# Moving the low-part subtractions of an attention and MLP kernel from GpSimd to VectorE

## The chip, the core and the metric

The kernel runs on one core of a Trainium2 chip. A core has four engines that matter here: TensorE (PE in the profile) multiplies matrices into PSUM; VectorE (DVE), ScalarE (ACT) and GpSimd (POOL) do elementwise work. Each engine takes its instructions in the order in which the program lists them, and waits at the head of its queue for what the instruction needs. SyncE (SP) issues most of the DMAs. The metric is the device time in microseconds; lower is better.

## What is computed

Attention over hashed buckets (2 batches, 8 heads, 768 tokens, 64 columns a head), then an MLP with squared ReLU (1536 tokens, 512 to 2048 to 512), then a mixture of 8 experts in which tokens are assigned greedily, 192 to each expert.

```python
def _attn_ref(q, k, v, proj):
    ...
    scores = scale * np.matmul(q, k.transpose(0, 1, 3, 2))
    scores = np.where(mask, scores, -1000000000.0)
    ...
    return np.matmul(attn, v).astype(np.float32)

def _moe_ref(x, w_in, w_out):
    h = np.maximum(x @ w_in, 0.0)
    return (h * h @ w_out).astype(np.float32)

def _moe2_ref(x, w_gate, w1, w2):
    logits = x @ w_gate
    order = np.argsort(-logits.flatten())
    ...
    for e in range(E):
        mask = assigned == e
        h = np.maximum(x[mask] @ w1[e], 0.0)
        out[mask] = h @ w2[e]
```

## The kernel before

Matrix products run in a rounded 32-bit type. To keep accuracy, each operand x is split into a high part hi, x rounded by ScalarE, and a low part lo = x − hi, and a product is the sum of three: hi·hi, hi·lo and lo·hi. `halve` (line 819) is the split of the MLP: its step 0 is the high part on ScalarE (line 821), its step 1 the low part, a subtraction of two SBUF operands on GpSimd (line 823).

The MLP works in 32 steps that the code calls slices s, listed in SEQ: each is one block f of 128 hidden columns (16 blocks) for one batch b of 768 tokens. `load` and `conv` (lines 798 and 803) bring a weight block and bring its 64-bit numbers into float32: L809 on ScalarE, then L811, L813, L815 and L817 on VectorE, each on 1024 columns. `split` (line 828) halves the three pieces of a block: 512 columns of w_out and two pieces of 256 of w_in.

The first 14 slices (PLAIN = 14) are plain: `first` multiplies (L874), evicts with ScalarE (L881) and VectorE (L883), and halves the hidden values (`chain`, line 876), 384 columns at a time. From slice 14 on slices go in pairs by a Strassen-like scheme with seven products for eight (`pairs`, L898), which needs sums of tokens and sums of weights. `tokens(b)` makes the token sums of batch b: for each of two column groups eight additions on VectorE (`tsum`, L861, in the tile tz) and four splits (`thalf`, line 863). `sums` (L841) makes the weight sums, whose split has 1024 columns. The products of a pair are evicted by L903 (ScalarE) and L905 (VectorE), squared by ScalarE (L909), halved by `chain`, and all slices go on to the second product (`mlp2`, L922). L939 adds up its results over the runs of SEQ.

Attention (L582 to L659) stands before the MLP, the router (L1312 to L1730, some of it already during the last slices) and the experts (L1877 to L2095) behind it.

No order is written out by hand. Each step goes to a planner, `Sched.add`, with its engine, a duration, what it depends on and a priority, lower first. `order` (line 107) plays the steps through on the engines, always starting what can start first, and emits the instructions of each engine in that order. A step with `port=True` may not run beside another such step in this play (line 150); GpSimd steps have it by default, of the VectorE steps the sums, and of the conversions only some. The real engines wait only for data, not for these marks. The priority of a slice's step of kind k is 500 + 10·s + MP[k] (line 986); tables like it (PR, EP, RP, FP) serve the other parts.

Of the kernel before, what the change touches and what calls it, by code (L numbers as in the profile page):

```python
# [232 lines left out]
XV = 8  # L233
XC = -13
PREP, PW, DL = -40.5, 0.8, 2.4
PREP1 = -10.5
LDP = (2, 0)
PR = {"S": 22, "mx": 1810, "ex": 846, "dn": -3872, "rec": -1060.5, "nrm": 1123.5, "tp": 28, "hi": -477.5, "lo": 542.5, "pv": 30, "oa": -524.5, "od": -1775, "pe": -35.5, "pa": -810.5, "pd": -1926}


def host_consts_a():
# [475 lines left out]
NS, STAG = 32, 3  # L717
PLAIN = 14
HALF = SEQ[PLAIN][1] + 1
MB = 500  # L720
LEAST = 3.4332275390625e-05
MP = {"ac": -17.5, "h1": -1100, "h2": 164.5, "ch": -3758, "hw": 146.5, "we": -678, "wn": -1359, "cv": -572.5, "sp": -2046.5, "sm": -72.5, "xs": -552, "sq": -3240.5, "lg": -473.5, "ev": -184.5, "lv": 292, "c0": 7498, "c1": 6337.5, "b0": 322, "b1": 3220.5}


def mlp(nc, S, ps, mem, ident, xhi, xlo, w_in, w_out, w_gate, wgt, x2d, L, att):
# [63 lines left out]
    def wo(f):  # L789
        return piece(S.unit(T["wo", f], "wo"), [512])  # L790
# [25 lines left out]
        else:  # L816
            V.scalar_tensor_tensor(x, x, LEAST, t.bitcast(F32), op0=OP.is_ge, op1=OP.mult)  # L817

    def halve(x, hi, lo, j):
        if j == 0:  # L820
            nc.scalar.activation(hi, x, AF.Copy)  # L821
        else:
            nc.gpsimd.tensor_tensor(lo, x, hi.bitcast(F32), op=OP.subtract)  # L823

    def flat(*a):
        return [x.rearrange("p " + "abc"[:len(x.shape) - 1].replace("", " ") + " -> p (" + "abc"[:len(x.shape) - 1].replace("", " ") + ")") for x in a]

    def split(f, k, j):
        if k == 2:
            halve(m(f)[:, 1], *wo(f), j)  # L830
        else:
            halve(m(f)[:, 0, 256 * k:256 * k + 256], *flat(*win(f, k)), j)

    def stg(p):
        return mem(S.unit(T["st", p], "wt"), [4, 2, 128])
# [40 lines left out]
    def chain(s, hf, j):  # L876
        hh, hl = hs(s)
        sl = slice(384 * hf, 384 * hf + 384)
        r = rs(s)[:, sl]
        if j == 0:  # L880
            nc.scalar.activation(r, hbank(s, hf), AF.Relu)  # L881
        elif j == 1:
            nc.vector.tensor_tensor(r, r, hbank(s, hf), op=OP.mult)  # L883
        else:
            halve(r, hh[:, sl], hl[:, sl], j - 2)

    def wbank(s, k):
        return ps(S.unit(T[k, s], "B"))[:, 0:384]
# [100 lines left out]
    def give(r, u, deps):  # L989
        S.add("NONE", 0.0, None, deps, rel=[(r, u)])  # L990

    def first(s):
        hd = []
        for hf in range(2):
            a = T["h", s, 0] if hf else None
            for c in range(4):
                a = S.add("PE", .52, lambda s=s, hf=hf, c=c: mlp1(s, hf, c), [*Wd[SEQ[s][1]], *[i for e in ends[4 * SEQ[s][0]:4 * SEQ[s][0] + 4] for i in e], a], prio=p(s, "h1") + hf, acq="B" if c == 0 else ())
                if c == 0:
                    T["h", s, hf] = a
                    T.setdefault(("l1", s), a)  # L1000
            L1.setdefault(SEQ[s][0], []).append(a)
            used.setdefault(SEQ[s][1], []).append(a)
            a = S.add("ACT", .37, lambda s=s, hf=hf: chain(s, hf, 0), [a, T.get(("hu", s))], prio=p(s, "ch"), acq=() if hf else ("h", "r0" if s < 2 else "r"))
            T.setdefault(("hu", s), a)
            b = S.add("DVE", .47, lambda s=s, hf=hf: chain(s, hf, 1), [a], prio=p(s, "ch"), rel=[("B", T["h", s, hf])])
            c = S.add("ACT", .41, lambda s=s, hf=hf: chain(s, hf, 2), [b], prio=p(s, "ch"))
            d = S.add("POOL", .956, lambda s=s, hf=hf: chain(s, hf, 3), [c], prio=p(s, "ch"))
            hd.append([c, d])
        give("r0" if s < 2 else "r", T["hu", s], [d, hd[0][1]])
        H[s] = hd  # L1010

    def tokens(b):

        out = {i: [] for i in range(1, 5)}
        pr = p(PLAIN, "xs") + 3 * (b == SEQ[PLAIN - 1][0])
        for c in range(2):
            A, V = {}, {}

            def add(j, deps):
                A[j] = S.add("DVE", .47, lambda c=c: tsum(b, c, j), deps, prio=pr, port=True)  # L1020

            def split2(i, deps):
                h = S.add("ACT", .41, lambda c=c: thalf(b, c, i, 0), deps, prio=pr)
                V[i] = S.add("POOL", .956, lambda c=c: thalf(b, c, i, 1), [h], prio=pr)
# [12 lines left out]
            add(6, [A[5], V[1]])
            add(7, [A[6]])
            split2(4, [A[7], *(used[HALF] if b == SEQ[PLAIN - 1][0] else ())])
            tfree[:] = [V[3], V[4], V[2]]  # L1040
        return out

    def pairs(s):
# [36 lines left out]
        for i, hf, d in ((0, 0, e2), (0, 1, z2), (1, 1, e4), (1, 0, e5)):  # L1080
            a = d if d == e5 else S.add("ACT", .41, lambda i=i, hf=hf: square(s + i, hf, AF.Relu), [d], prio=p(s, "sq"))
            a = S.add("ACT", .41, lambda i=i, hf=hf: square(s + i, hf, AF.Square), [a], prio=p(s, "sq"))
            h = S.add("ACT", .41, lambda i=i, hf=hf: chain(s + i, hf, 2), [a], prio=p(s, "ch"))
            l = S.add("POOL", .956, lambda i=i, hf=hf: chain(s + i, hf, 3), [h], prio=p(s, "ch"))
            H.setdefault(s + i, [None, None])[hf] = [h, l]
        for i in range(2):
            give("r", T["hu", s + i], [x[1] for x in H[s + i]])
# [86 lines left out]
    for f in range(16):  # L1174
# [6 lines left out]
        d = S.add("DMA", 2.9, None, [a], prio=MB + 10 * s, lat=1.8)  # L1181
        T["tm", f] = a = S.add("ACT", .95, lambda f=f: conv(f, 0), [d, *gate], prio=p(s, "cv"), acq=("wt", "mi", "mo"))
        for j in range(1, 5):
            a = S.add("DVE", dur[j - 1], lambda f=f, j=j: conv(f, j), [a], prio=p(s, "cv"), port=f < 2 or j == 1, rel={3: [("wr", T["wr", f])], 4: [("wt", T["tm", f])]}.get(j, ()))
        T["cv", f] = a

        def parts(key, n, fn, deps, sm=(), acq=()):
            i = S.add("ACT", .2 + .00073 * n, lambda: fn(0), deps, prio=p(s, "sp"), acq=acq)
            T.setdefault(key, i)
            return [i, S.add("POOL", .1 + .00225 * n, lambda: fn(1), [i, *sm], prio=p(s, "sp"))]  # L1190

        def win_(f, k, key):
            Wd[f] += parts(key, 256, lambda j: split(f, k, j), [a], acq=() if key in T else key[0])
# [13 lines left out]
        else:  # L1207
# [1002 lines left out]
```

## Time and profile before

| | us |
|---|---|
| median of three runs | 794.42 (793.69 to 794.68) |
| the profiled execution | 796.18 |
| its span, first to last instruction | 794.4 |
| TensorE busy | 762.6 |
| VectorE busy | 575.5 |
| ScalarE busy | 460.6 |
| GpSimd busy | 432.0 |

Busy time is the time in which an instruction of the engine runs. The mean granted TensorE clock is 0.972 of full speed. TensorE has two speeds, 1.2 and 2.4 GHz; a granted clock below 1.00 in a stretch says that part of it ran at the lower. Stages by time: attention to about 270, the MLP from about 250 to 560, the router to about 590, the experts to the end.

### The profile page before, as it was taken

The page shows a single profiled execution, that of the slowest core. Times are in us where ns is not written, and L with a number is a line of the kernel's source. Part 1 is how long each engine was busy: PE and PEld are TensorE (multiplying, and loading weights), DVE is VectorE, ACT ScalarE, POOL GpSimd, SP SyncE. Part 2 cuts the span into 40 slices and gives each one's busy share as a digit, 9 for nine tenths or more (in the row PEclk, how much of TensorE's full clock was granted, in tenths as well). Part 3 has the DMA queues.
Part 4 walks back from the last instruction along what each step waited for, and adds up shares of the span by engine and source line. Part 5 has one row for each costly group of instructions (what it writes and reads, how often), then busy time and mean ns, then how long its engine had stood idle before and what let it go on. Part 6 is the DMA issues. An engine that isn't in the chain of part 4 may idle for free.

```text
span 794.4 us, 14089 instructions
## 1 busy us (share of the span) xinstructions
PE 762.6 (96%) x4970; PEld 666.9 (84%) x4970; DVE 575.5 (72%) x1173; ACT 460.6 (58%) x949; POOL 432.0 (54%) x446
## 2 busy tenths in 40 slices
PE   8899999999999989999799999999999999999996
PEld 5678888888887889988688999898679899888885
DVE  6879999999999787499867666316876768754432
ACT  7789999999997663543457565544332312333332
POOL 3668778778798776576837665317421412231110
PEclk9999999999999999999999999998689999999998
DMA  8969659556701312210202310101166385897001
GB/s 181 238 131 196 131 113 190 130 120 144 178 12 54 105 54 67 93 54 29 78 22 84 106 54 1 65 15 67 68 206 208 117 277 191 306 334 267 21 8 33
DMA packets 77734, 94.34 MB, mean 119 GB/s; under 512 B 29632, under 2 KB 56640, under 8 KB 77664
## 3 DMA queue, kind: packets, MB, share of 16 engines
q1 hardware_dynamic: 75616, 87.16, 39.8%
q0 software_dynamic: 2048, 6.29, 2.6%
q8 instruction: 39, 0.64, 0.3%
q14 instruction: 31, 0.25, 0.1%
HBM read 63.55 MB, written 6.29 MB: 88 GB/s over the span
## 4 chain that ended last, share of the span: by engine, by line
PE 67%; DVE 13%; issue 8%; ACT 5%; POOL 3%; DMA 2%; SPq 1%; POOLq 0%; ACTq 0%; DVEq 0%
PE psS L922 9%; PE psS L582 7%; PE psS L1959 6%; PE psTP L898 4%; PE psO L898 4%; PE psTP L618 3%; DVE tz L861 3%; PE psm L922 2%; PE psTP L922 2%; PE psS L2000 2%; PE psO L874 2%; PE psTP L874 2%; PE psm L618 2%; PE psO L618 2%; PE psTP L639 1%
## 5 line engine op out<-in xcount | busy, mean ns | idle before, releaser
L823 POOL TENSOR_TENSOR r<-f,r 128x384 fp32r<-128x384 f32 (+3 forms) x112 | 137.5, 1251 | 106.0 <-ACT r L821 79.7
L610 POOL TENSOR_TENSOR f<-f 128x768 f32<-128x768 f32 x96 | 142.8, 1489 | 26.4 <-PE psTP L618 11.1
L922 PE MATMUL psS<-r 128*128 128x512 f32 x384 | 103.9, 406 | 0.2 <-DVE f L939 0.2
L598 DVE TENSOR_REDUCE f<-psS 128x1 f32<-128x768 f32 x96 | 90.5, 944 | 1.8 <-PE psS L582 1.6
L582 PE MATMUL psS<-r 128*128 128x384 f32 x384 | 88.1, 350 | 2.6 <-issue 1.6
L601 ACT ACTIVATE f<-psS,f 128x768 f32<-128x768 f32 x96 | 87.7, 913 | 3.4 <-DVE f L598 1.2
L922 PEld LDWEIGHTS psS<-r 128*128 128x128 f32 x384 | 73.8, 196 | 13.5 <-DVE f L939 0.5
L821 ACT ACTIVATE r<-f 128x384 fp32r<-128x384 f32 (+3 forms) x112 | 56.2, 532 | 37.4 <-DVE f L817 19.0
L1959 PE MATMUL psS<-ff,rf 128*128 128x192 f32 x400 | 76.5, 336 | 0.0
L1903 POOL DMA_INDIRECT ff<-x2d,ix x16 | 24.5, 1528 | 89.9 <-DVE ix L1728 49.9
L582 PEld LDWEIGHTS psS<-r 128*128 128x128 f32 x384 | 65.2, 188 | 8.7 <-ACT f L601 6.1
L1959 PEld LDWEIGHTS psS<-ff,rf 128*128 128x128 f32 x400 | 66.0, 193 | 1.6 <-DVE ff L1930 0.3
L2082 POOL DMA_INDIRECT out_dram<-ff,ix x16 | 16.6, 1035 | 89.5 <-DVE ff L2093 67.2
L630 DVE TENSOR_TENSOR p<-psTP,p 128x384 fp32r<-128x384 f32 x92 | 49.7, 546 | 2.9 <-ACT p L626 2.0
L626 ACT ACTIVATE p<-psTP 128x384 fp32r<-128x384 f32 x92 | 45.1, 502 | 10.7 <-PE psTP L618 9.0
L1879 DVE TENSOR_TENSOR ff<-rf,ff 128x1024 fp32r<-128x1024 f32 x22 | 26.9, 1222 | 32.5 <-ACT ff L1877 32.5
L1877 ACT ACTIVATE ff<-rf 128x1024 fp32r<-128x1024 f32 x22 | 23.3, 1057 | 45.5 <-PE psS L2030 36.3
L618 PE MATMUL psTP<-ident,f 128*128 128x128 f32 x276 | 45.1, 274 | 1.6 <-POOL f L610 1.2
L618 PEld LDWEIGHTS psTP<-ident,f 128*128 128x128 f32 x276 | 33.7, 140 | 7.9 <-issue 1.8
L909 ACT ACTIVATE f<-f 128x384 f32<-128x384 f32 x63 | 31.7, 520 | 13.4 <-DVE f L905 12.9
L604 POOL TENSOR_SCALAR f<-f 128x1 f32<-128x1 f32 x96 | 22.6, 235 | 30.5 <-ACT f L601 25.2
L874 PE MATMUL psTP<-r 128*128 128x384 f32 x150 | 29.7, 347 | 3.6 <-DVE f L883 3.6
(454 smaller groups left out, 1956.2 us busy)
## 6 DMA issues: line engine op xcount, KB each, us to landing
rf<-in_moe_w_dram SPq DMA_DIRECT2D x60, 512.0 KB, 6.4
r<-r SPq DMA_DIRECT2D x90, 192.0 KB, 4.2
f<-in_moe_w_in_dram SPq DMA_DIRECT2D x16, 512.0 KB, 3.8
f<-in_moe_w_out_dram SPq DMA_DIRECT2D x16, 512.0 KB, 4.6
r<-r SPq DMA_DIRECT2D x15, 384.0 KB, 4.0
f<-in_q_dram SPq DMA_DIRECT2D x8, 384.0 KB, 5.7
f<-in_k_dram SPq DMA_DIRECT2D x8, 384.0 KB, 6.3
f<-in_v_dram SPq DMA_DIRECT2D x8, 384.0 KB, 4.7
```

The lines of the kernel that those rows point to most:

```text
L582: nc.tensor.matmul(sbank(u)[:, hf, 0:384], T["q", (pr, h)][:, n, 128 * i:128 * i + 128], T["k", (pr, h)][:, n, 384 * hf:384 * hf + 384], s ...
L598: nc.vector.tensor_reduce(col(0, u), sbank(u)[:, :, 0:384], axis=AX.XY, op=OP.max, negate=True)
L601: nc.scalar.activation(P(u).rearrange("p (a b) -> p a b", a=2), sbank(u)[:, :, 0:384], AF.Exp, bias=col(0, u), accum_out=col(1, u))
L610: nc.gpsimd.tensor_tensor(Pn(u), P(u), col(3, u).to_broadcast([128, 768]), op=OP.mult)
L618: nc.tensor.transpose(tp(u, g)[:, j], Pn(u)[:, 128 * c:128 * c + 128], ident)
L630: nc.vector.tensor_tensor(tl, tp(u, g), th.bitcast(F32), op=OP.subtract)
L821: nc.scalar.activation(hi, x, AF.Copy)
L823: nc.gpsimd.tensor_tensor(lo, x, hi.bitcast(F32), op=OP.subtract)
L874: nc.tensor.matmul(hbank(s, hf), w[:, c % 2], y[:, x, sl], start=(c == 0 and i == 0), stop=(c == 3 and i == 2))
L898: nc.tensor.matmul(wbank(s, k), w[x][:, c], y[z][:, c], start=st and c == i == 0, stop=c == 1 and i == 2, skip_group_check=not st)
L922: nc.tensor.matmul(abank(i), a[:, t], w, start=(f == RUNS[r][1][0] and j == 0), stop=(f == RUNS[r][1][-1] and j == 2))
L1959: nc.tensor.matmul(abank(n)[:, j], raw(p, g)[:, 0, 256 * c + 128 * j:256 * c + 128 * j + 128], xT(p)[:, c], start=(c == 0), stop=(c == 3))
```

## The change

Low parts go to VectorE instead of GpSimd in three places: the hidden values of slices from 14 on (LOS), the weight pieces and weight sums of blocks from 10 on (WLO), and all token sums. The planner's durations for them change with the engine, and they are marked as users of the port, as are now all steps of a conversion. The token sums of batch b get the due time of that batch's first paired slice (14 and 18); before, both had that of slice 14, batch 1 three units behind. All tables of priorities (PREP1, PR, MP, EP, RP, FP) have new numbers; of MP this core shows all.

```diff
+LOS, WLO = 14, 10
...
-MP = {"ac": -17.5, "h1": -1100, "h2": 164.5, "ch": -3758, "hw": 146.5, "we": -678, "wn": -1359, "cv": -572.5, "sp": -2046.5, "sm": -72.5, "xs": -552, "sq": -3240.5, "lg": -473.5, "ev": -184.5, "lv": 292, "c0": 7498, "c1": 6337.5, "b0": 322, "b1": 3220.5}
+MP = {"lw": -774.5, "ac": 24.5, "h1": -252.5, "h2": 273.5, "ch": -3545, "hw": 253.5, "we": -1093, "wn": -1773, "cv": -742, "sp": -3335.5, "sm": -1005, "xs": -292.5, "sq": -2724, "lg": -93.5, "ev": 307.5, "lv": 292, "c0": 8976.5, "c1": 6037.5, "b0": 230.5, "b1": 3618}
...
-    def halve(x, hi, lo, j):
+    def halve(x, hi, lo, j, e=None):
         if j == 0:
             nc.scalar.activation(hi, x, AF.Copy)
         else:
-            nc.gpsimd.tensor_tensor(lo, x, hi.bitcast(F32), op=OP.subtract)
+            (e or nc.gpsimd).tensor_tensor(lo, x, hi.bitcast(F32), op=OP.subtract)
...
+    def we(f):
+        return nc.gpsimd if f < WLO else nc.vector
+
     def split(f, k, j):
         if k == 2:
-            halve(m(f)[:, 1], *wo(f), j)
+            halve(m(f)[:, 1], *wo(f), j, we(f))
         else:
-            halve(m(f)[:, 0, 256 * k:256 * k + 256], *flat(*win(f, k)), j)
+            halve(m(f)[:, 0, 256 * k:256 * k + 256], *flat(*win(f, k)), j, we(f))
...
     def thalf(b, c, i, j):
-        halve(tf((None, 1, 2, 0, 1)[i]), *(x[:, c] for x in tb(b, i)), j)
+        halve(tf((None, 1, 2, 0, 1)[i]), *(x[:, c] for x in tb(b, i)), j, nc.vector)
...
-            halve(r, hh[:, sl], hl[:, sl], j - 2)
+            halve(r, hh[:, sl], hl[:, sl], j - 2, nc.gpsimd if s < LOS else nc.vector)
...
+    def low(s, hf, deps):
+        pool = s < LOS
+        return S.add("POOL" if pool else "DVE", .956 if pool else .43, lambda: chain(s, hf, 3), deps, prio=p(s, "ch" if pool else "lw"), port=True)
...
-        pr = p(PLAIN, "xs") + 3 * (b == SEQ[PLAIN - 1][0])
+        pr = p(next(i for i in range(PLAIN, NS) if SEQ[i][0] == b), "xs")
...
-                V[i] = S.add("POOL", .956, lambda c=c: thalf(b, c, i, 1), [h], prio=pr)
+                V[i] = S.add("DVE", .47, lambda c=c: thalf(b, c, i, 1), [h], prio=pr, port=True)
...
-            l = S.add("POOL", .956, lambda i=i, hf=hf: chain(s + i, hf, 3), [h], prio=p(s, "ch"))
+            l = low(s + i, hf, [h])
...
-            a = S.add("DVE", dur[j - 1], lambda f=f, j=j: conv(f, j), [a], prio=p(s, "cv"), port=f < 2 or j == 1, rel={3: [("wr", T["wr", f])], 4: [("wt", T["tm", f])]}.get(j, ()))
+            a = S.add("DVE", dur[j - 1], lambda f=f, j=j: conv(f, j), [a], prio=p(s, "cv"), port=True, rel={3: [("wr", T["wr", f])], 4: [("wt", T["tm", f])]}.get(j, ()))
...
-            return [i, S.add("POOL", .1 + .00225 * n, lambda: fn(1), [i, *sm], prio=p(s, "sp"))]
+            return [i, S.add("POOL" if f < WLO else "DVE", .1 + .00225 * n if f < WLO else .05 + .00105 * n, lambda: fn(1), [i, *sm], prio=p(s, "sp"), port=True)]
...
-            Sd[q] = parts(("wS", q), 1024, lambda j, q=q: halve(*flat(stg(q), *wS(q)), j), [x, T["wx", q]])
+            Sd[q] = parts(("wS", q), 1024, lambda j, q=q: halve(*flat(stg(q), *wS(q)), j, we(2 * q + 1)), [x, T["wx", q]])
```

## Rows read from the trace of the kernel before

**Rows 1.** Busy us (instructions) of PE, PEld, DVE, ACT, POOL; clock, DMA share, GB/s.

```profile
60.00:240.00 180.00, 179.33 (x1170) 160.10 (x1169) 169.56 (x350) 167.96 (x375) 146.04 (x164) 1.00 0.62 133
270.00:295.00 25.00, 22.88 (x116) 21.41 (x116) 19.37 (x22) 14.50 (x31) 16.17 (x20) 0.94 0.25 85
295.00:340.00 45.00, 45.00 (x229) 41.00 (x228) 28.25 (x30) 21.47 (x44) 27.96 (x24) 1.00 0.21 71
340.00:402.00 62.00, 55.05 (x257) 48.33 (x256) 57.31 (x61) 26.96 (x56) 46.44 (x34) 0.94 0.15 52
402.00:480.00 78.00, 77.80 (x390) 69.98 (x389) 53.10 (x62) 48.48 (x97) 46.88 (x36) 1.00 0.20 68
480.00:540.00 60.00, 59.74 (x330) 53.60 (x329) 19.98 (x35) 28.29 (x58) 21.49 (x18) 1.00 0.08 29
540.00:590.00 50.00, 48.51 (x526) 35.13 (x525) 38.09 (x105) 21.02 (x41) 27.23 (x24) 0.73 0.27 91
```

**Rows 2.** Waits, whole execution: who waited for whom, us in total, times, longest.

```profile
PE psTP L874 <- DVE f L883: 3.9, 4, 2.1
PE psTP L898 <- ACT f L903: 3.1, 1, 3.1
PE psTP L898 <- DVE f L905: 2.0, 1, 2.0
ACT f L821 <- DVE tz L861: 17.9, 9, 4.7
```

**Rows 3.** Timelines of four engines, 382 to 388: start, us, instruction, idle before it.

```profile
383.69 1.97 POOL L823 TENSOR_TENSOR f<-tz,f 128x384 fp32r<-128x384 f32 x1
385.69 1.15 DVE L861 TENSOR_TENSOR tz<-tz,r 128x384 f32<-128x384 f32 x2 [0.89 <-POOL f L823]
386.87 0.52 ACT L821 ACTIVATE f<-tz 128x384 fp32r<-128x384 f32 x1 [4.68 <-DVE tz L861]
387.83 0.69 PE L898 MATMUL psTP<-f,r 128*128 128x384 f32 x1 [3.13 <-ACT f L903]
```

**Rows 4.** Busy VectorE us (count) of L861, L841, L813, L815 alone, 340 to 402.

```profile
340.00:402.00 62.00, 21.11 (x20) 0.94 0.15 52
340.00:402.00 62.00, 5.88 (x7) 0.94 0.15 52
340.00:402.00 62.00, 5.88 (x3) 0.94 0.15 52
340.00:402.00 62.00, 5.87 (x3) 0.94 0.15 52
```

**Rows 5.** Three lines' instructions, whole execution: shortest/median/longest in ns.

```profile
L861 DVE TENSOR_TENSOR tz<-tz,r x12: 546/888/2155, 287.2 to 394.2; 128x384 f32<-128x384 f32 x12
L841 DVE TENSOR_TENSOR f<-f x20: 409/649/1395, 355.2 to 487.2; 128x256 f32<-128x256 f32 x20
L813 DVE SCALAR_TENSOR_TENSOR f<-f x16: 1214/1921/2868, 237.4 to 478.6; 128x1024 int32<-128x1024 int32 x16
```

**Rows 6.** GpSimd's groups, 340 to 402, token sums: count, busy us, mean ns, idle before.

```profile
L823 POOL TENSOR_TENSOR f<-tz,f 128x384 fp32r<-128x384 f32 x9 | 14.3, 1593 | 1.9 <-ACT f L821 1.8
L823 POOL TENSOR_TENSOR r<-tz,r 128x384 fp32r<-128x384 f32 x3 | 5.3, 1770 | 0.0
```

**Rows 7.** GpSimd's groups, 402 to 480, in the same columns.

```profile
L823 POOL TENSOR_TENSOR r<-f,r 128x384 fp32r<-128x384 f32 x20 | 28.2, 1430 | 20.7 <-ACT r L821 10.7 <-PE psTP L898 5.2 <-issue 4.7
L823 POOL TENSOR_TENSOR r<-f,r 128x1024 fp32r<-128x1024 f32 x3 | 7.2, 2408 | 5.1 <-ACT r L821 5.1
L823 POOL TENSOR_TENSOR r<-f,r 128x512 fp32r<-128x512 f32 x5 | 6.7, 1332 | 6.8 <-ACT r L821 6.8
L823 POOL TENSOR_TENSOR r<-f,r 128x256 fp32r<-128x256 f32 x8 | 6.0, 758 | 0.0
```

**Rows 8.** Two of VectorE's groups, 402 to 480, in the same columns.

```profile
L815 DVE SCALAR_TENSOR_TENSOR f<-f 128x1024 int32<-128x1024 int32 x6 | 9.4, 1575 | 0.2
L905 DVE TENSOR_TENSOR f<-psTP,f 128x384 f32<-128x384 f32 x8 | 4.4, 552 | 11.9 <-PE psTP L898 9.4 <-ACT f L903 2.5
```

More of the change, by code (lines that the diff above doesn't have):

```diff
@@ L235 @@
 PREP, PW, DL = -40.5, 0.8, 2.4
-PREP1 = -10.5
+PREP1 = 3
 LDP = (2, 0)
-PR = {"S": 22, "mx": 1810, "ex": 846, "dn": -3872, "rec": -1060.5, "nrm": 1123.5, "tp": 28, "hi": -477.5, "lo": 542.5, "pv": 30, "oa": -524.5, "od": -1775, "pe": -35.5, "pa": -810.5, "pd": -1926}
+PR = {"S": 22, "mx": 1264, "ex": -144, "dn": -3726, "rec": -2216.5, "nrm": 1537.5, "tp": 27.5, "hi": -226, "lo": 175, "pv": 29.5, "oa": -1881.5, "od": -1440.5, "pe": -31.5, "pa": -522, "pd": -2310}
 def host_consts_a():
@@ L1006, in first @@
             c = S.add("ACT", .41, lambda s=s, hf=hf: chain(s, hf, 2), [b], prio=p(s, "ch"))
-            d = S.add("POOL", .956, lambda s=s, hf=hf: chain(s, hf, 3), [c], prio=p(s, "ch"))
+            d = low(s, hf, [c])
             hd.append([c, d])
@@ L1242, in mlp @@
     return [ld[n] for n in range(12)], st, [i for f in range(16) for i in [*Wd[f], *Sd.get(f // 2, [])]], zone_(L1[0])
-EP = {"fr": -48.5, "lr": -962.5, "row": 360, "col": -240, "cp": -71.5, "ca": 1048, "gp": 330}
+EP = {"fr": -277, "lr": -125, "row": -996.5, "col": 1318, "cp": -12, "ca": 817.5, "gp": 1047}
 CP = (5, 2, 4, 2, 1, 0)
@@ L1252 @@
 ND = 4
-RP = {"fr": 1566.5, "se": -5127.5, "oh": -545.5, "G": 3844.5, "A": 2231, "lr": 310.5, "pf": -940.5, "id": 161, "gp": 2059, "sq": 30.5, "G1": 2135.5, "A1": -374, "ei": -381, "up": 1389.5}
+RP = {"fr": 2161.5, "se": -5096.5, "oh": -968.5, "G": 3516, "A": 2902.5, "lr": 1192.5, "pf": -346.5, "id": 443.5, "gp": 2614, "sq": 196, "G1": 1462.5, "A1": -62.5, "ei": -284.5, "up": 1188.5}
 ACT_TILES = {12: (10, 11), 9: (8,), 6: ()}
@@ L1832, in squeeze @@
         st["L"], st["alive"], st["tok"] = a, None, e1
-FP = {"ga": -278.5, "xp": 2407.5, "xe": 2225, "m1": 2482, "re": -1938.5, "m2": 979, "ye": -532.5, "yt": 1964.5, "yo": 1379, "sc": 1112.5, "sp": 1289, "mr": 1136.5}
+FP = {"ga": -1074.5, "xp": 2624, "xe": 2280.5, "m1": 2986.5, "re": -1156.5, "m2": 1829, "ye": -1710.5, "yt": 2599.5, "yo": 2225.5, "sc": 1064, "sp": 545, "mr": 2334}
 AP = 5
```

## The prediction

> **What bounds the kernel now.** I read the table by stage first [rows 1]. PE is the long pole everywhere: in attention it works 179.33 of 180 us, from 295 to 340 all of 45, from 402 to 540 all but 0.5 of 138. No other engine can make those stretches shorter, only longer. Time is lost in two stretches of the MLP. From 340 to 402 PE works 55.05 of 62 us and its clock is granted at 0.94, so part of the stretch ran at the lower of its two levels: 62 − 55.05 = 6.95 us idle plus 0.06 × 62 = 3.7 us of clock, 10.7 us in all. From 270 to 295 it is 2.1 us idle plus 0.06 × 25 = 1.5 us, 3.6 us in all. The other place where PE is slow, 540 to 590 (clock 0.73), is the router, a chain of small steps that the change does not move.
>
> Then the list of waits [rows 2]: PE waits for evictions, L883 and L905 on VectorE and L903 on ScalarE, and ScalarE for L861, the token sums on VectorE. In order of time around the longest gap [rows 3]: a low part of a token sum ran on GpSimd from 383.69 for 1.97 us; VectorE sat idle 0.89 us until it ended, then ran four sums; ScalarE stood 4.68 us with a token high part at the head of its queue, behind which the eviction L903 was waiting; PE started 3.13 us late. So in 340 to 402 the chain runs through VectorE and GpSimd, and VectorE is at 57.31 of 62 us, 92%.
>
> Last, why VectorE is so full. The table by line gives 21.11 us for 20 sums, 1.06 us each, 5.88 for three L813, 5.87 for three L815, 5.88 for seven L841 [rows 4], while the shortest of them take 0.546, 1.214 and 0.409 us [rows 5] (L815 is shaped as L813, and I take its 1.214). The excess is 21.11 − 10.9 = 10.2, 2.2, 2.2 and 3.0, together 17.6 us. GpSimd's low parts are stretched too: those of token sums take 1593 to 1770 ns [rows 6]. The operations of both engines named here have two inputs in SBUF; the eviction L905, with one in PSUM, stays at 552 ns [rows 8]. The Trainium skill ("SBUF — State Buffer", Who interferes with whom) says that such a VectorE instruction and a GpSimd one exclude each other for a whole instruction; the 0.89 us of rows 3 agrees.
>
> **The change, part by part.** *Token sums.* All 16 low parts leave GpSimd; 12 of them are in 340 to 402, 9 × 1.593 + 3 × 1.770 = 19.6 us of GpSimd's 46.44 [rows 1, 6]. VectorE pays 12 × 0.546 = 6.6 us (a sum of the same shape, both inputs in SBUF). If the excess goes with GpSimd's time, 19.6/46.44 of 17.6 = 7.4 us comes back, net −0.8 us of VectorE. The ends: nothing comes back (+6.6), all of it does (−11.0). I take −0.8, since 58% of GpSimd's time in this stretch stays (slices below 14, weights below 10). On the chain itself the step gets shorter, 1.6 us on GpSimd to 0.55, and crosses between engines once less.
>
> *Their due time.* Batch 1's sums were due 3 units after batch 0's; a slice is 10 units, and now they are due with slice 18 instead of 14. Of 32 sums 20 start in the stretch [rows 4]; batch 0 goes first, so the 16 of batch 1 are all among them, at 0.546 to 1.06 us each 8.7 to 16.9 us of VectorE that no longer stands ahead of the first pair. What is late next is slice 18: the first pair starts near 383 [rows 3] and 18 slices run to 540, 8.7 us each, so the sums get some 35 us more, into 402 to 420, where VectorE still has room (53.10 of 78 [rows 1]).
>
> *Hidden and weight low parts.* From 402 to 480 GpSimd runs 36 low parts, nearly all of which move: 20 of 384 columns, 3 of 1024, 5 of 512, 8 of 256 [rows 7]. On VectorE, with 0.68 for 512 read off the line between the others (an estimate): 20 × 0.546 + 3 × 1.214 + 5 × 0.68 + 8 × 0.409 = 21.2 us. Against it stands the excess there: 6 × (1.575 − 1.214) = 2.2 us for L815 [rows 5, 8], about as much for each of the two other long steps of a conversion, some for L841: 8 us, an estimate from that row. From 480 on VectorE has 40 idle us of 60 [rows 1]; 16 moved parts fit.
>
> *The sum on VectorE, as a check.* 340 to 480: 57.3 + 53.1 = 110.4 us now; −7.4 − 8 + 6.6 + 21.2 gives 122.8. At the 92% at which it ran flat out, that is 133 us where there are 140: VectorE lets the stage shrink by about 7 us, not by the whole 10.7. I take 7.0, with ends 0 (the excess stays: 138 us) and 10.7.
>
> *270 to 295.* No low part is moved here. The 3.9 us of waits for L883, the longest 2.1 [rows 2], come where three sums stood ahead of it. The sums are now due later (xs −552 to −292.5) and conversions sooner. I take half of 3.6, 1.8 us; ends 0 and 3.6.
>
> *Turns.* More VectorE steps are marked as users of the shared port, so the planner no longer lays them beside GpSimd's. That only orders each queue, and adds no wait between the engines. I cost it at nothing beyond the above; the excess that could go with it is in the ends.
>
> *New order elsewhere.* All tables of due times are new. In attention there is nothing to win (0.7 us of 180) and up to 2 us to lose, by the nearest row of a disturbed stretch, 270 to 295. Router and experts keep their work: 0, ends ±3 us, about the size of the stage losses above. No DMA is moved; the expert weights start when the MLP closes, and so move with it.
>
> **Sum.** −7.0 − 1.8 = −8.8 us. The profiled execution took 796.18 us, 794.4 of it span: 787.4. The median of the runs is 794.42, 1.8 lower, so on that scale 785.6, which I predict.
>
> **Rivals.** *The turns work and all comes back* (13%): 10.7 + 3.6, and a few us of the router's 0.73 clock because GpSimd is free earlier: −14 to −17, 777.5 to 780. For it: 52 token and hidden low parts leave GpSimd, and those of six weight slices. Against: the check sum.
>
> *The change does not do what it says* (15% for a small gain, 8% for none): order is no wait, conversions and the low parts left on GpSimd go on meeting, the excess stays, and only the later due time helps: −1.6 to −5, 789.4 to 793, or nothing, 794.4. The Trainium skill ("Perfetto Trace Analysis", Optimizing Scalar/DVE Operations) warns that moving work between the two might not help because they share a read port; the stretched rows agree that they share it, but a VectorE low part would hold it for 0.55 us and a GpSimd one runs 1.43 [rows 5, 7].
>
> *VectorE becomes the bound from 402 to 480* (17%, slower): 53.1 − 8 + 21.2 = 66.3 us there, and with batch 1's 16 sums and 8 low parts (24 × 0.546 = 13.1) 79.4 of 78. Evictions L905 then stand behind conversions in one queue, the next pair's banks come free late, and PE idles. It decides once VectorE passes the 92% of 340 to 402; by that stretch's own loss, 10.7 of 62, it costs 17% of 78 = 13.4 us. With 8.8 won before it: +4.6, 799. The Trainium skill ("Perfetto Trace Analysis", Optimizing Scalar/DVE Operations) advises taking work off a saturated VectorE, which speaks for this rival. Against: half of batch 1's part can run before 402, which gives 72.8, and 295 to 340 has 16 us of VectorE idle.
>
> **How the numbers follow.** Forecast (−5 to −12) 47%, larger 13%, small gain 15%, none 8%, slower 17%. About 0.2%, 1.6 us, is what can be told from no change: faster 0.75, same 0.08, slower 0.17. For 8 in 10 the range takes in the larger gain and no change, and leaves the slower cases beyond: 777.5 to 796.0.
>
> **What would show it.** Right: from 340 to 402 PE above 60 us and its clock at 1.0; sums at a mean of 0.55 to 0.8 us; L811 to L817 near their shortest from 400 on; GpSimd falling from 54 instructions between 402 and 540 [rows 1] to a few; PE still full to the end of the MLP, which ends near 531 instead of 540; router and experts as long as before. Wrong: idle PE behind L905 or a low part between 400 and 480 with VectorE above 92%; sums still above 1 us; attention longer than now; or the gain of the MLP given back after 540.

## The result and the profile after

The changed kernel takes 784.82 us (median, 783.3 to 786.42), the one before 794.06 us beside it: a ratio of 0.9885, interval [0.986, 0.991], 9.2 us faster. The prediction was 785.6, 8.8 us faster, in a range from 777.5 to 796.0 that takes in no change as well. The two profiled executions differ by more, 796.18 and 783.99 us (spans 794.4 and 782.2): the one of before lies 2.1 us above its median, the one of after 0.8 below. So 2.9 of the 12.2 us between the traces are scatter. The file grew: L823 is now L824, L861 is L865, L841 is L845, L813 is L814, L883 is L887, L898 is L902, L905 is L909, L922 is L926, L1903 is L1911, L2082 is L2090.

The stages of the changed kernel, in the columns of [rows 1]:

```profile
270.00:295.00 25.00, 23.52 (x119) 20.67 (x119) 22.87 (x25) 15.20 (x30) 17.25 (x13) 1.00 0.26 84
295.00:340.00 45.00, 45.00 (x236) 41.83 (x235) 29.25 (x33) 24.57 (x48) 28.04 (x31) 1.00 0.21 71
340.00:402.00 62.00, 59.68 (x293) 52.42 (x292) 57.83 (x83) 29.87 (x61) 26.73 (x19) 1.00 0.15 52
402.00:480.00 78.00, 78.00 (x388) 69.99 (x387) 60.76 (x97) 48.56 (x94) 0.00 (x0) 1.00 0.20 68
480.00:540.00 60.00, 59.27 (x356) 53.16 (x354) 28.82 (x67) 31.58 (x66) 10.25 (x10) 1.00 0.13 49
540.00:590.00 50.00, 49.68 (x602) 38.42 (x602) 39.16 (x128) 17.26 (x33) 18.80 (x19) 0.86 0.44 144
```

Between 340 and 402 PE works 59.68 of 62 us at full clock, where it had 55.05 at 0.94 [rows 1]: 2.3 us lost instead of 10.7. Between 270 and 295 it is 1.5 instead of 3.6. VectorE is as full as it was, 57.83 us, but with 83 instructions instead of 61. GpSimd has 19 there instead of 34, and none at all from 402 to 480.

The waits of the changed kernel over the whole execution, which answer to [rows 2]:

```profile
PE psO L1929 <- DMA ff<-x2d,ix: 3.5, 1, 3.5
PE psTP L902 <- DVE f L909: 1.3, 1, 1.3
PE psm L878 <- DVE f L887: 1.2, 2, 0.7
PE psTP L878 <- DVE f L887: 1.0, 2, 0.8
ACT f L822 <- DVE tz L865: 20.7, 8, 4.2
```

PE's waits of 3.1 and 2.0 us at the first pairs and its 3.9 us for L883 have shrunk to 1.3 and 2.2. ScalarE still waits for token sums, 20.7 us in all; only PE no longer waits behind it. The longest wait of PE is now one of 3.5 us for a gather, in the experts; before, its wait for a gather was 2.0 us.

The lines' own times (count: shortest/median/longest in ns), answering to [rows 5], and the low parts that are now VectorE's:

```profile
L865 DVE TENSOR_TENSOR tz<-tz,r x12: 544/931/1645, 281.0 to 392.1; 128x384 f32<-128x384 f32 x12
L845 DVE TENSOR_TENSOR f<-f x20: 411/415/427, 346.6 to 474.0; 128x256 f32<-128x256 f32 x20
L814 DVE SCALAR_TENSOR_TENSOR f<-f x16: 1210/1219/1648, 237.2 to 467.1; 128x1024 int32<-128x1024 int32 x16
L824 DVE TENSOR_TENSOR f<-tz,f x12: 543/549/1095, 286.2 to 394.9; 128x384 fp32r<-128x384 f32 x12
```

Weight sums and conversions run close to their shortest: L845 has a median of 415 ns where it had 649, L814 of 1219 where it had 1921. The token sums are stretched as before: a median of 931 where it was 888. All those that run from 340 to 402, in the columns of [rows 4], take 0.98 us each where they took 1.06:

```profile
340.00:402.00 62.00, 18.69 (x19) 1.00 0.15 52
```

Where the time went, by marks in the traces (start of the last product of attention with V, of the first and the last product of a pair, of the first expert product; then the span):

| kernel | attention's end | first pair | last pair | first expert | span | pairs | router | experts |
|---|---|---|---|---|---|---|---|---|
| before | 276.6 | 382.4 | 532.3 | 587.2 | 794.4 | 149.9 | 54.9 | 207.2 |
| after | 272.6 | 375.4 | 519.3 | 571.9 | 782.2 | 143.9 | 52.6 | 210.3 |
| e1_engines_back | 275.3 | 378.9 | 527.9 | 580.5 | 791.2 | 149.0 | 52.6 | 210.7 |
| e2_old_tables | 277.6 | 382.8 | 526.3 | 578.7 | 787.7 | 143.5 | 52.4 | 209.0 |
| e3_emit_pool | 273.9 | 376.7 | 522.3 | 574.5 | 785.1 | 145.6 | 52.2 | 210.6 |
| e4_emit_dve | 277.8 | 380.3 | 526.7 | 580.5 | 787.8 | 146.4 | 53.8 | 207.3 |
| e5_due_back | 272.8 | 375.7 | 519.5 | 572.1 | 782.9 | 143.8 | 52.6 | 210.8 |
| e8_old_att | 276.8 | 376.7 | 520.2 | 572.8 | 783.8 | 143.5 | 52.6 | 211.0 |
| e9_old_router_experts | 272.7 | 375.6 | 519.4 | 572.5 | 780.8 | 143.8 | 53.1 | 208.3 |
| e10_port_back | 273.1 | 378.1 | 521.7 | 573.1 | 784.3 | 143.6 | 51.4 | 211.2 |
| e11_due_alone | 279.5 | 385.4 | 532.2 | 585.9 | 793.5 | 146.8 | 53.7 | 207.6 |
| e13_old_fp | 272.9 | 375.9 | 519.7 | 574.0 | 821.7 | 143.8 | 54.3 | 247.7 |
| e14_tok_dve | 278.8 | 381.2 | 525.8 | 579.3 | 788.4 | 144.6 | 53.5 | 209.1 |
| e15_rest_dve | 277.0 | 382.8 | 532.6 | 587.5 | 795.6 | 149.8 | 54.9 | 208.1 |

The first pair starts 7.0 us earlier, the pairs take 6.0 less and the router 2.3 less; the experts take 3.1 more: −12.2 us.

### The profile page after: what moved, and what is told of

It is laid out like the page before. It is cut to its first block, busy times and chain, and to the rows that moved or that the text cites. A ratio compares the mean times of both kernels' runs of the same rounds, so it can differ in the third digit from the quotient of the medians.

```text
span 782.2 us, 14059 instructions
## 1 busy us (share of the span) xinstructions
PE 755.5 (97%) x4979; PEld 663.1 (85%) x4979; DVE 588.1 (75%) x1243; ACT 462.3 (59%) x949; POOL 341.6 (44%) x376
## 4 chain that ended last, share of the span: by engine, by line
PE 64%; DVE 17%; issue 9%; ACT 5%; DMA 2%; POOL 1%; SPq 0%; POOLq 0%; ACTq 0%; DVEq 0%
PE psS L926 9%; PE psS L1967 7%; PE psS L582 5%; DVE p L630 4%; PE psTP L902 4%; PE psm L902 4%; DVE f L598 4%; PE psTP L878 3%; PE psO L926 3%; PE psS L2008 2%; PE psTP L926 2%; PE psm L878 2%; DVE tz L865 2%; PE psTP L618 2%; PE psO L1339 1%
## 5 line engine op out<-in xcount | busy, mean ns | idle before, releaser
L926 PE MATMUL psS<-r 128*128 128x512 f32 x384 | 100.6, 395 | 0.3 <-DVE f L943 0.3
L824 POOL TENSOR_TENSOR r<-f,r 128x384 fp32r<-128x384 f32 (+3 forms) x58 | 74.8, 1312 | 55.6 <-ACT r L822 52.4
L926 PEld LDWEIGHTS psS<-r 128*128 128x128 f32 x384 | 70.5, 188 | 13.6 <-DVE f L943 1.1
L582 PEld LDWEIGHTS psS<-r 128*128 128x128 f32 x384 | 64.2, 188 | 10.1 <-ACT f L601 7.1
L2090 POOL DMA_INDIRECT out_dram<-ff,ix x16 | 22.2, 1385 | 112.1 <-DVE ff L2101 67.2
L1475 POOL TENSOR_SCALAR f<-f,mx 128x768 bf16<-128x768 f32 (+1 forms) x3 | 8.3, 2755 | 134.5 <-ACT f L1461 134.5
L1887 DVE TENSOR_TENSOR ff<-rf,ff 128x1024 fp32r<-128x1024 f32 x22 | 26.9, 1222 | 31.4 <-ACT ff L1885 31.4
L1911 POOL DMA_INDIRECT ff<-x2d,ix x16 | 19.5, 1218 | 68.8 <-DVE cq L1803 28.8
L824 DVE TENSOR_TENSOR r<-f,r 128x384 fp32r<-128x384 f32 (+3 forms) x54 | 30.5, 582 | 18.0 <-ACT r L822 17.9
```

What stands on the lines that cost most here:

```text
L582: nc.tensor.matmul(sbank(u)[:, hf, 0:384], T["q", (pr, h)][:, n, 128 * i:128 * i + 128], T["k", (pr, h)][:, n, 384 * hf:384 * hf + 384], s ...
L824: (e or nc.gpsimd).tensor_tensor(lo, x, hi.bitcast(F32), op=OP.subtract)
L926: nc.tensor.matmul(abank(i), a[:, t], w, start=(f == RUNS[r][1][0] and j == 0), stop=(f == RUNS[r][1][-1] and j == 2))
```

## The experiments

Each result is the ratio to the kernel before, timed beside it on the same chip, with its 95% interval. On the chips of the experiments the kernel before took 796.4 to 796.8 us, so 0.001 is 0.8 us.

**The first question** was whether the engine or the order does it. Theory 1: low parts on GpSimd hold the port that VectorE's operations need, and moving them frees VectorE. Theory 2: the new order, due time and tables do it, and the engine is a detail.

*e1_engines_back*: all low parts planned for and issued to GpSimd again; due time, marks and tables stay.

```diff
-LOS, WLO = 14, 10
+LOS, WLO = 32, 16
...
-                V[i] = S.add("DVE", .47, lambda c=c: thalf(b, c, i, 1), [h], prio=pr, port=True)
+                V[i] = S.add("POOL", .956, lambda c=c: thalf(b, c, i, 1), [h], prio=pr)
...
-        halve(tf((None, 1, 2, 0, 1)[i]), *(x[:, c] for x in tb(b, i)), j, nc.vector)
+        halve(tf((None, 1, 2, 0, 1)[i]), *(x[:, c] for x in tb(b, i)), j)
```

> All low parts go back to GpSimd and the planner knows it; due times, marks and tables stay as changed. Theory 1 (the engine of the low parts is the cause: fewer GpSimd operations hold the port that VectorE needs): the sums L865 go back to a mean of about 1.0 us, PE is idle again in the stretch before the first pairs, 792 to 798 us, that is 7 to 13 more than the changed kernel's 784.8. Theory 2 (new order and due times do it, the engine hardly matters): 784 to 788.

Measured: 0.9928 [0.9908, 0.9947], 791.14 us, between the two theories: 5.7 us of the gain stay with all low parts of the MLP on GpSimd. The pairs take 149.0 us, as before; the gain lies ahead of them. From 340 to 402 PE is as full as in the changed kernel; from 402 to 480 it loses 4.0 us, and two of its waits, which end at 479.5 and 489.3, are for low parts on GpSimd (columns of [rows 1], then of [rows 2]):

```profile
340.00:402.00 62.00, 60.13 (x296) 53.09 (x295) 53.12 (x62) 29.22 (x56) 42.85 (x34) 1.00 0.16 52
402.00:480.00 78.00, 74.00 (x367) 65.56 (x367) 49.28 (x60) 48.31 (x99) 46.52 (x39) 1.00 0.20 68
PE psS L926 <- POOL r L824: 2.4, 1, 2.4
PE psm L902 <- POOL r L824: 1.4, 1, 1.4
```

*e2_old_tables*: the changed kernel with all priority tables of before.

```diff
-PREP1 = 3
+PREP1 = -10.5
...
-MP = {"lw": -774.5, "ac": 24.5, "h1": -252.5, ...
+MP = {"lw": -3758, "ac": -17.5, "h1": -1100, ...
```

(PR, EP, RP and FP likewise, each as the diff of the change has them on its minus side.)

> The changed kernel with the priority tables of before (the new key lw gets the number that ch had); engines, marks and due time stay as changed. Theory 1: most of the 9.2 us stays, 784 to 789. Theory 2: the gain is lost, 791 to 797; attention's last score product goes back from 254.4 to about 257.6 us under both, since only the tables can have moved it.

Measured: 0.9915 [0.9885, 0.9946], 789.44 us. Most of the gain needs no new table; the pairs take 143.5 us.

*e3_emit_pool*: the changed kernel's own plan, but the low parts are issued to GpSimd in the places that were planned for VectorE.

```diff
-            (e or nc.gpsimd).tensor_tensor(lo, x, hi.bitcast(F32), op=OP.subtract)
+            nc.gpsimd.tensor_tensor(lo, x, hi.bitcast(F32), op=OP.subtract)
```

> The changed kernel's own plan, every queue in the order that was planned for VectorE, but the low parts are issued to GpSimd. Theory 1: the stretching returns (sums at a mean over 0.9 us, conversions' steps over 1.5 us) and the low parts take 1.0 us and more instead of 0.55: 795 to 806 us. Theory 2: within 3 us of the changed kernel, 782 to 788.

Measured: 0.9888 [0.9854, 0.9923], 787.06 us, the changed kernel's own ratio. Theory 1 had said 795 to 806. Its trace from 270 to 295 and from 340 to 402, in the columns of [rows 1]:

```profile
270.00:295.00 25.00, 23.52 (x120) 20.79 (x119) 21.71 (x23) 15.73 (x32) 19.31 (x14) 1.00 0.21 68
340.00:402.00 62.00, 59.60 (x293) 52.20 (x292) 57.31 (x67) 29.71 (x59) 50.28 (x36) 1.00 0.15 52
```

And its token sums there, in the columns of [rows 4]:

```profile
340.00:402.00 62.00, 20.78 (x21) 1.00 0.15 52
```

GpSimd is busier than before, 50.28 us, the sums are as stretched as in the changed kernel (0.99 us each, there 0.98), and yet PE works 59.60 of 62 us. So the port is not what PE waits for once the order is another. What the other order gives can be read from PE's list at the first pair, in the kernel before (first two rows, L898) and in e3 (the others, L902):

```profile
383.50 1.20 PE L898 MATMUL psO<-r 128*128 128x384 f32 x6
387.83 2.29 PE L898 MATMUL psTP<-f,r 128*128 128x384 f32 x6 [3.13 <-ACT f L903]
377.80 1.20 PE L902 MATMUL psTP<-r 128*128 128x384 f32 x6
378.84 1.55 PE L926 MATMUL psS<-r 128*128 128x512 f32 x6
380.60 1.31 PE L902 MATMUL psTP<-f,r 128*128 128x384 f32 x6 [0.21 <-DVE f L909]
```

Before, the pair's third group of six multiplications follows the second directly and has to wait for an eviction. In e3, as in the changed kernel, six multiplications of the MLP's second product (L926) stand between them, 1.55 us of work for PE while evictions run. That this is what counts in the new order is read from the traces; no run tries it alone.

*e4_emit_dve*: the reverse. The kernel of before with its own plan, but those low parts that the change moves are issued to VectorE.

```diff
-            halve(r, hh[:, sl], hl[:, sl], j - 2)
+            halve(r, hh[:, sl], hl[:, sl], j - 2, nc.gpsimd if s < LOS else nc.vector)
```

(likewise in `split`, `thalf` and for the weight sums, as in the change)

> The kernel of before with its own plan, in which the low parts stand where GpSimd would have done them, but those that the change moves are issued to VectorE: the move alone, not planned for. Theory 1: sums fall to a mean below 0.8 us and 3 to 8 us are won, 786 to 791. Theory 2: nothing is won or it gets slower, since VectorE is given 35 us more work in an order that was not made for it: 794 to 802.

Measured: 0.9946 [0.993, 0.9963], 792.23 us: the move alone, in an order not made for it, brings 4.3 us. Neither theory holds alone. Its trace from 402 on, same columns:

```profile
402.00:480.00 78.00, 76.92 (x382) 68.53 (x381) 63.15 (x99) 48.51 (x97) 0.00 (x0) 1.00 0.20 68
480.00:540.00 60.00, 58.99 (x340) 52.99 (x339) 25.52 (x55) 30.17 (x62) 4.06 (x2) 1.00 0.11 40
```

PE loses 1.1 and 1.0 us here, where it lost 0.2 and 0.3 before [rows 1]. In the first stretch it waits twice 0.5 us for L943 on VectorE. In the second, 0.6 us are a wait of the router (L1451), which starts earlier in this trace, and e14 below, without this load on VectorE, loses as much there (59.02 us).

**The second question** was which part of the order. Theory D puts it on the due time of batch 1's sums, Theory T on the marks of the conversions.

*e5_due_back*: the changed kernel with the old due time; *e11_due_alone*: the kernel before with the new one.

```diff
-        pr = p(next(i for i in range(PLAIN, NS) if SEQ[i][0] == b), "xs")
+        pr = p(PLAIN, "xs") + 3 * (b == SEQ[PLAIN - 1][0])
```

(e11 is the same line the other way, in the kernel before)

> The changed kernel, with the token sums of both batches due with slice 14 again, batch 1 three units behind; engines, marks and tables stay. Theory D (the later due time of batch 1 is what empties VectorE ahead of the first pairs): the first pair starts later than the changed kernel's 375.4 us by 3 to 7, and 788 to 792. Rival (the due time is a detail, the rest of the order and the engine carry the gain): 783.5 to 786.5, first pair at 375 to 377.

> The kernel of before with the one line on the due time of batch 1's sums and nothing else. Theory D: 3 to 5 us faster than before, 789 to 791 on its scale of 794. Rival: within 1.5 us of before, 792.5 to 795.5.

Measured: e5 0.9855 [0.982, 0.989], 785.16 us. With the new tables the old due time gives the same order of instructions on every engine, so this is the changed kernel once more: 0.9855 and 0.9885 are two measurements of one program, and ratios of different sets of runs that are less than 0.003 apart say nothing here. e11 gave 0.9938 [0.9914, 0.9962], 791.94 us, 4.9 us faster by one line. In its trace attention ends 2.9 us later though nothing of attention was edited: 2.6 us of that are lost in the first 13 us. The pairs take 146.8 us instead of 149.9. This execution took 795.25 us, the slowest of its ten, and shows little of the gain: PE's wait of 3.1 us for L903 is gone, but in its place PE waits 3.1 us for L905.

*e8_old_att* and *e10_port_back*: the changed kernel with attention's old tables, and with the old marks.

```diff
-PREP1 = 3
+PREP1 = -10.5
...
-... port=True, rel={3: [("wr", T["wr", f])], ...
+... port=f < 2 or j == 1, rel={3: [("wr", T["wr", f])], ...
```

(the first hunk, with PR as before, is e8; the second is e10)

> The changed kernel with attention's tables (PR, PREP1) of before. In the profiled executions attention's last product ended at 276.6 us before and 272.6 after; with these tables and the changed engines it was 277.6. If the tables give that: 787.5 to 789.5, and 277 again. If it was the scatter of single executions, or hidden by what comes next: 784 to 786.

> The changed kernel, with only those steps of a conversion marked as users of the port that were marked before. Theory T (turns in the plan keep the conversions from being stretched): L814 to L818 go back from a mean of 1.29 to 1.37 us to over 1.5, and 786.5 to 790. Rival (marks only shift the plan a little, the engines meet as they did): means below 1.45 us and 783 to 786.5.

Measured: e8 0.9886 [0.9852, 0.992], 788.1 us; e10 0.9887 [0.9849, 0.9926], 787.46 us. Both are the ratio of the changed kernel's first measurement. Beside e5, the same program timed together with them on one chip, they are 2.9 and 2.3 us slower, by four runs each and with intervals that overlap: a cost of 2 to 3 us is neither shown nor excluded. The seven traces with attention's new tables end attention at 272.6 to 275.3 us, the seven with the old ones at 276.6 to 279.5, so the tables do move it by some 4 us. But in e8 the first pair starts at 376.7 us, only 1.3 later than in the changed kernel: the plain slices' products had been done in between. The marks on the conversions change their means little (L814 at 1.39 us, in the changed kernel 1.29), and the time by no more than this comparison can tell.

**The third question**, after e4: which of the moved low parts? Theory C: the chain of the token sums, which at each step waits for a low part on GpSimd. Theory P: the port, so that their number counts.

*e14_tok_dve*: the kernel before with its own plan; only the 16 low parts of token sums are issued to VectorE.

```diff
-    def halve(x, hi, lo, j):
+    def halve(x, hi, lo, j, e=None):
...
-            nc.gpsimd.tensor_tensor(lo, x, hi.bitcast(F32), op=OP.subtract)
+            (e or nc.gpsimd).tensor_tensor(lo, x, hi.bitcast(F32), op=OP.subtract)
...
-        halve(tf((None, 1, 2, 0, 1)[i]), *(x[:, c] for x in tb(b, i)), j)
+        halve(tf((None, 1, 2, 0, 1)[i]), *(x[:, c] for x in tb(b, i)), j, nc.vector)
```

*e15_rest_dve*: as e4_emit_dve, but the token sums' low parts stay on GpSimd: the other 54 alone.

```diff
-        halve(tf((None, 1, 2, 0, 1)[i]), *(x[:, c] for x in tb(b, i)), j, nc.vector)
+        halve(tf((None, 1, 2, 0, 1)[i]), *(x[:, c] for x in tb(b, i)), j)
```

> The kernel of before with its own plan; only the 16 low parts of token sums are issued to VectorE. Theory C (the chain of token sums, which waits at each step for a low part on GpSimd, is what holds the first pairs): most of what e4_emit_dve won, 3 to 5 us, 791 to 793 where before is 796. Theory P (the port: what counts is how many of GpSimd's operations leave): 16 of the 70 moved ones, so about 1 us, 795.

> The kernel of before with its own plan; only the low parts of hidden values from slice 14 and of weights from block 10 are issued to VectorE, the token sums' stay on GpSimd. Theory C: nothing is won, since PE is full where these 54 stand: 795 to 797.5 where before is 796. Theory P: 3 to 4 us are won, 792 to 793.

Measured: e14 0.99 [0.9878, 0.9923], 789.55 us, 8.0 us by the ratio, more than either theory said. e15 0.9979 [0.996, 0.9998], 794.66 us: 1.7 us (by the interval 0.2 to 3.2), hardly to be told from no change. So the place counts, as Theory C says, and not the number, as Theory P says. Whether it is the chain that makes the place count is another question. Two stretches of e14, in the columns of [rows 1], then the wait of its ScalarE for the sums, in the columns of [rows 2], and its sums alone from 340 to 402, in the columns of [rows 4]:

```profile
270.00:295.00 25.00, 22.07 (x118) 20.29 (x119) 20.57 (x24) 15.41 (x31) 15.58 (x20) 1.00 0.26 85
340.00:402.00 62.00, 59.24 (x289) 51.96 (x288) 55.33 (x77) 30.76 (x60) 34.98 (x25) 1.00 0.15 52
```

```profile
ACT f L821 <- DVE tz L861: 12.4, 8, 4.2
340.00:402.00 62.00, 14.96 (x20) 1.00 0.15 52
```

The stretch from 340 to 402 in e15, and the waits of its PE:

```profile
340.00:402.00 62.00, 55.34 (x264) 48.31 (x263) 58.73 (x66) 27.91 (x58) 44.32 (x32) 0.97 0.15 52
```

```profile
PE psTP L878 <- DVE f L887: 3.9, 4, 2.2
PE psTP L902 <- ACT f L907: 3.1, 1, 3.1
PE psTP L902 <- DVE f L909: 1.8, 1, 1.8
```

In e14 PE is nearly full and ScalarE's wait for the sums falls from 17.9 [rows 2] to 12.4 us. VectorE's 20 sums take 14.96 us, from 21.11 [rows 4]; with L813, L815 and L817, three of each, it is 26.7 us from 37.5, and the 12 low parts cost 7.8. In e15 every one of the waits of [rows 2] stands where it was, though 54 low parts are gone from GpSimd. And e4, which is e14 and e15 together, is 3.7 us slower than e14 alone, by ratios whose intervals do not meet: by that, the 54 cost time where the order does not expect them. The two profiled executions, of 787.8 and 788.4 us, do not show these 3.7 us.

PE and ScalarE run the same list of instructions in e14 as before, so the gain can be followed along it. PE gains 1.5 us near 293, 1.8 between 340 and 370, and 5.6 between 382 and 402, where its two waits at the first pair stand. The wait for L903 falls from 3.13 to 1.84 us: VectorE's 0.89 us of waiting for a low part on GpSimd [rows 3] is gone, and the L813 ahead of the sums takes 1.21 us instead of 1.92. The wait of 2.0 us for the later of two evictions L905 is gone, and one of 0.6 us for the earlier is new. This is what VectorE ran between the two, beside one L939, before (five rows) and in e14 (six):

```profile
390.24 1.56 DVE L817 SCALAR_TENSOR_TENSOR f<-f 128x1024 f32<-128x1024 f32 x1
391.72 1.37 DVE L861 TENSOR_TENSOR tz<-r,tz 128x384 f32<-128x384 f32 x1
393.01 1.23 DVE L841 TENSOR_TENSOR f<-f 128x256 f32<-128x256 f32 x1
394.17 1.65 DVE L861 TENSOR_TENSOR tz<-tz,r 128x384 f32<-128x384 f32 x1
395.74 0.94 DVE L841 TENSOR_TENSOR f<-f 128x256 f32<-128x256 f32 x1
387.83 1.22 DVE L817 SCALAR_TENSOR_TENSOR f<-f 128x1024 f32<-128x1024 f32 x1
388.96 0.55 DVE L823 TENSOR_TENSOR f<-tz,f 128x384 fp32r<-128x384 f32 x1
389.43 0.55 DVE L861 TENSOR_TENSOR tz<-r,tz 128x384 f32<-128x384 f32 x1
389.90 0.42 DVE L841 TENSOR_TENSOR f<-f 128x256 f32<-128x256 f32 x1
390.24 0.55 DVE L861 TENSOR_TENSOR tz<-tz,r 128x384 f32<-128x384 f32 x1
390.70 0.42 DVE L841 TENSOR_TENSOR f<-f 128x256 f32<-128x256 f32 x1
```

VectorE waits for nobody in either list. The five operations that both have take 6.75 us before and 3.16 in e14, where one low part of 0.55 us is added. Before, GpSimd ran low parts without a break from 388.72 to 396.40; in e14 it was idle from 381.70 to 389.72. So in the old order the port does count, in this place: by stretching what stands ahead of an eviction that PE needs. The chain and the stretching both go when these low parts leave GpSimd, and no run parts the two.

**The fourth question** was the experts' 3.1 us. In the changed kernel's timeline GpSimd's queue looks like this (start, duration, engine and operation; in brackets the idle time ahead of it), and the last three rows are what VectorE ran meanwhile:

```profile
608.28 6.21 POOL L2090 DMA_INDIRECT out_dram<-ff,ix  x1 [22.72 <-DVE ix L1736]
614.79 0.97 POOL L1911 DMA_INDIRECT ff<-x2d,ix  x1 [0.31 <-issue]
607.99 2.26 DVE L1606 TENSOR_SCALAR ff<-ff,mx 128x1152 bf16<-128x1152 f32 x3
610.17 1.21 DVE L1887 TENSOR_TENSOR ff<-rf,ff 128x1024 fp32r<-128x1024 f32 x1
611.31 3.08 DVE L1606 TENSOR_SCALAR ff<-ff,mx 128x1152 bf16<-128x1152 f32 x4
```

A scatter stands ahead of the gather that the next expert needs.

*e13_old_fp* takes back FP alone, *e9_old_router_experts* takes back EP, RP and FP.

```diff
-FP = {"ga": -1074.5, "xp": 2624, "xe": 2280.5, ...
+FP = {"ga": -278.5, "xp": 2407.5, "xe": 2225, ...
```

> The changed kernel with the experts' priorities (FP) of before. From the first expert product to the end it took 210.3 us where the kernel before took 207.2, and in the trace a scatter of 6.21 us stood ahead of a gather on GpSimd, for which PE waited 3.5 us. If the new FP does that: the stretch falls to about 207.5 and 2 to 4 us are won over the changed kernel, a ratio to before of 0.982 to 0.985, 781 to 783 on the scale of 794. If the delay comes from the router's new order or the earlier start: 210 again, a ratio of 0.986 to 0.989.

> The changed kernel with the priorities of router and experts (EP, RP, FP) of before. From the last product of a pair to the first of the experts it took 54.9 us before and 52.6 after. If the new EP and RP do that: 54 to 55 us again, and with the experts back at 207.5 a ratio to before of 0.985 to 0.988. If these 2 us come from GpSimd's being free or VectorE's being ahead when the router starts: 52.5 us, and a ratio as of e13_old_fp, 0.982 to 0.985.

Measured: e13 1.0325 [1.0298, 1.0351], 823.36 us, 26 us slower, which no theory had. The experts take 247.7 us, with PE at 10.93 of 20 us in one stretch while the DMA engines are at 0.93:

```profile
760.00:780.00 20.00, 10.93 (x65) 9.69 (x65) 6.97 (x24) 3.47 (x5) 4.99 (x7) 0.60 0.93 312
```

Router and experts share the engines and their priorities are compared with each other, so one of the tables alone may put all of the router's steps ahead or behind; that this is what happens in e13, and which step suffers, is not shown and stays open. e9 gave 0.9852 [0.9827, 0.9877], 783.95 us. Its experts take 208.3 us, and in its timeline the gather stands first again:

```profile
608.07 2.63 POOL L1911 DMA_INDIRECT ff<-x2d,ix  x1 [21.89 <-DVE ix L1736]
611.00 4.08 POOL L1911 DMA_INDIRECT ff<-x2d,ix  x1 [0.30 <-issue]
```

Against the changed kernel's 0.9885 and 0.9855 that is no difference that can be told. Its router takes 53.1 us, so by this one trace most of the router's gain does not hang on the new EP and RP.

## Why the prediction was right, and where its steps failed

**The stretch and its size: right, the size in part by luck.** PE's losses from 340 to 402 and from 270 to 295 were named as what could be won. Of 10.7 us 8.4 came back (7.0 had been taken), of 3.6 us 2.1 (1.8 had been taken); PE reached 59.68 us at a clock of 1.00 where above 60 had been named as a sign. But the 7.0 was what VectorE's total seemed to allow, and e3 has PE as full (59.60) with VectorE and GpSimd as busy as before (57.31 and 50.28 us). The total did not set the size. The 1.8 was half of the loss, taken without a working.

**Token sums: right in place, mis-sized.** The prediction put them at −0.8 us, the net of VectorE's busy time. Done alone in the old order (e14) they are worth 8.0 us, nearly the whole gain. Two things were too small in it. First, what comes back: 7.4 us of excess were taken, and in e14 the sums and conversions from 340 to 402 give back 10.8 us. Second, and more, where it comes back. The working priced the engine's time and mentioned the chain in one sentence; but the time falls ahead of L903 and L905, the evictions for which PE waits, once through the chain (sum, high part on ScalarE, low part on GpSimd at 1.6 to 1.8 us, a further sum, and in ScalarE's queue the eviction behind it [rows 3]) and once through the stretched steps ahead of L905. e15 is the counter-test: without the token sums, all the rest of the move leaves these waits as they were. In one reading of this the prediction was wrong: VectorE's 0.89 us of [rows 3] are not the port. That sum writes over a tile tz that GpSimd's low part reads, and waited for it to end; what speaks for the port are the stretched rows.

**The due time: wrong as a step of this change.** The prediction had batch 1's sums leave the crowded stretch for 402 to 420. With the new tables the line changes no instruction's place (e5), and the changed kernel's last token sum starts before 395, as before. Alone, in the old order, it is worth 4.9 us (e11), the upper end of the 1.6 to 5 us that the prediction's rival of a small gain gave it.

**So the parts do not add up.** Token sums alone 8.0, due time alone 4.9, the new order with GpSimd still doing the work (e3) 8.9, all together 9.2 (or 11.5, by e5's ratio). They go for one and the same loss, PE's idle time and the lower clock ahead of and in the first pairs: of 14.3 us in the two stretches 5.7 are left in e14, 3.9 in e3 and 3.8 in the changed kernel. The token sums alone and the new order alone each take most of it. The prediction added terms of different stretches only, and its check by VectorE's total capped the sum, so it did not count one loss twice; that helped it to come out.

**VectorE's total: right as a sum, not the bound.** 122.8 us were worked out for 340 to 480; it is 57.83 + 60.76 = 118.6. From 402 to 480 VectorE is at 78%, so the rival in which it becomes the bound did not come. A small part of it exists: e4, with this load in an order that was not made for it, loses 1.1 us of PE there, most of it in two waits for L943.

**The stretched operations: half right.** From 400 on conversions run at their shortest, as forecast. The token sums were forecast at 0.55 to 0.8 us and stay at 18.69/19 = 0.98 us: the new order puts them among the low parts of the plain slices, which stay on GpSimd. That was the rival "the change does not do what it says", true for this line and without weight for the time: e3 shows sums as stretched as here and PE full, so in the new order the stretching is not the bound. In the old order it was part of it (e14).

**Turns: nothing that can be told.** Without the marks (e10) the ratio is that of one measurement of the changed kernel, and 0.003 above that of the other.

**Elsewhere: right within the ends.** Attention's end moved by 4 us, and in e8's trace its products only trade places with those of the plain slices; the ratio leaves room for some 2 to 3 us. The router's 2.3 us shorter and the experts' 3.1 us longer stretch lie within the ±3 us given, and nearly cancel.

**What stays open.** e1 and e3 have the same engines, due times and tables; they differ in the order that the planner makes when it believes the moved low parts to be short and VectorE's (the hidden ones then go by the priority lw and not by ch). e3 is the faster, 0.9888 against 0.9928, intervals that overlap at the edge. The traces put the difference from 402 on, where PE works 74.00 of 78 us to 480 in e1 and 77.60 in e3, and e1 waits for GpSimd. Which place in the order does it was not tried alone. Nor was the chain of the token sums parted from the stretching that its low parts cause.

## What to carry to other kernels

Price a moved step by the chain in which it stands, by what waits behind it in a third engine's queue and by what it stretches just ahead of such a wait, not only by the time of the two engines; 16 well placed instructions brought 8.0 us, 54 others 1.7 (0.2 to 3.2). When several edits aim at one idle stretch, try each alone and expect them to overlap. A move that is planned and a move that is only issued are two experiments: planning in one engine and issuing in the other (e3, e4) separated order from engine in two runs. Tables of priorities that are compared with each other are not taken back one by one: one of three cost 26 us, all three nothing.

## What the hardware showed

The issue of the indirect DMA L2090 on GpSimd takes 0.9 to 1.0 us in most of its places (shortest 898 ns, median 983), but 6.21 us at 608.28, beside the rows of L1606 on VectorE. It ended at 614.49, 0.1 us after the last of them (611.31 + 3.08 = 614.39). In e9 the two gathers end in the same way: the first, of 2.63 us, at 610.70, 0.1 us after a row of L1606 (610.57), the second, of 4.08 us, at 615.08, 0.1 us after the last L1606 there (614.98). The Trainium skill ("SBUF — State Buffer", SBUF: two separate sides) says that a VectorE instruction in one of its two-port modes keeps GpSimd from writing descriptors, and the ends right behind the rows agree. Whether L1606 runs in such a mode no row says; it takes 0.81 us for 1152 columns where the subtraction L1887 takes 1.21 for 1024. These traces add that one issue can be held over many instructions: in the changed kernel over seven L1606 with L1887 among them, which follow one another without a gap, and in e9 over the 0.27 us for which VectorE was idle ahead of its last L1606. L1887 itself gives no clear answer: the first gather of e9 ended while it ran, the scatter of the changed kernel did not.
